# Linear attention with two expert stages on one core: y computed by tokens, the router's logits as eight more columns a head, one weight conversion at another place

## The chip, the cores and the metric

One core of one Trainium2 chip runs the whole program. TensorE (PE in the profile) multiplies into PSUM, VectorE (DVE), ScalarE (ACT) and GpSimd (POOL) work on the results, and SyncE (SP) issues most transfers. The metric is device time in microseconds (us), lower is better; where two numbers are compared, it is that of whole executions.

## The reference, cut to what matters

```
batch, n_heads, seq, head_dim = (4, 8, 768, 48)
f = 1.0 / (1.0 + np.exp(-f_logit))
for t in range(S):
    state = f[:, :, t, :, None] * state + np.einsum('bhd,bhe->bhde', k[:, :, t], v[:, :, t])
    y[:, :, t] = np.einsum('bhd,bhde->bhe', q[:, :, t], state)
x = np.ascontiguousarray(y.transpose(0, 2, 1, 3)).reshape(B * S, H * D)     # 3072 x 384
logits = x @ w_gate + modality_bias[modality_id]                            # 8 experts
e_idx = np.argmax(logits, axis=1)
out[mask] = gate_w[mask, None] * (np.maximum(x[mask] @ w1[e], 0.0) @ w2[e]) # for each expert e
return (1 / (1 + np.exp(-(x @ w_gate2))) * (x @ w_val)) @ w_out             # second stage, d_ff 1536
```

So there is a linear attention with a decay per feature, a top-1 mixture of eight experts that is routed by the attention's output, and a gated layer on all 3072 tokens.

## The kernel before, in words

The recurrence runs over 24 tiles of 128 tokens (6 chunks of 4 batches), in a loop whose iterations are called slots here. Heads stand in pairs: head 2·pr+j has 64 partitions, of which 48 differ. All products of this stage are in fp32, so each matmul instruction leaves two weight loads and two matmuls in the trace (a count of 16 there is 8 instructions). For tile i the names in the code and the profile are: `c` the running sum of the log decays (L966, 8 instructions), `rg` its two exponentials, `kqT` the decayed k and q, `turn` the transposed k (L1003, 4 transposes), `kt` its copy, `a` the products k·q (L1015, 16), `am` those after the causal mask, `u` the tile's contribution k·v to the state (L1033, 8), `s` the state.

The output y is made by features. `att_ys` (L1058, 8 instructions) multiplies the state with q, `att_y` (L1071, 8) adds v times `am`, both into the PSUM tile `yT`; ScalarE copies it (L1076); one slot later `att_x` (L1102, 8 instructions of 104 columns) multiplies the turned y with `wr`, which holds an identity and the router's weights side by side, and so gives both the rows by tokens and four partial logits a token. ScalarE copies these apart (`rows` L1105, `lg` L1106). The logits of a group of tiles (ROUTE) are summed on VectorE (`lgs`, L1108), and then a chain of small VectorE steps, dealt out one at a time between the other work (`tick`), finds expert, rank and place. Rows go to DRAM (`store_rows`), and a table of places is kept on chip.

The order of every engine is that of the code. A slot i issues a(i), ys(i-1), x(i-2), y(i-1), c(i+2), u(i), turn(i+1). The loads are issued in order by SP: f(i+5), kq(i+4), v(i+3), each into a ring of 4 or 5 buffers. Between them stand conversions of the last stage's float64 weights to float32 in halves: a load of 768 KB, one ScalarE step (L856), four VectorE steps (L861, L865, L869, L873), a store of 384 KB. CONV says in which slots of the recurrence one begins; others have their places in the expert stage.

The first two expert blocks (`slot32`, here block 0 and block 1) start from the tokens of the first 18 tiles: their ids are taken from the table (`take`, L351), their rows gathered from DRAM by POOL (`xg`, L403) and turned (`xT`, L739), while the last slots of the recurrence still run. After them come the other expert blocks and the gated layer.

Of the kernel before, what the change touches and what calls it, by code (L numbers as in the profile page):

```python
# [10 lines left out]
F32 = mybir.dt.float32  # L11
# [11 lines left out]
P = 128  # L23
# [5 lines left out]
E = 8  # L29
# [3 lines left out]
XW = 2 * D + E  # L33
# [10 lines left out]
CONV = (3, 7, 11, 15)  # L44
GROUPED = 17
PUT = (9, 13, 17)
# [14 lines left out]
def kernel(  # L61
# [3 lines left out]
    att_fv: bass.AP,  # L65
# [41 lines left out]
    wr = ctile([P, 4, XW], F32, "wr")  # L107
# [39 lines left out]
    def setup_early(causal):  # L147
# [12 lines left out]
        nc.gpsimd.memset(wr, 0.0)  # L160
        for j in range(2):
            nc.gpsimd.tensor_copy(
                out=wr[:, :, j * D:(j + 1) * D],
                in_=ident[:, 64 * j:64 * j + D].rearrange("p (o d) -> p o d", o=1).to_broadcast([P, 4, D]),
            )
# [7 lines left out]
    def load_router():  # L173
        wsrc = w_router.rearrange("(p j d) e -> j d p e", j=2, d=D)
        nc.sync.dma_start(out=wr[0:D, :, 2 * D:XW], in_=wsrc[0])
        nc.sync.dma_start(out=wr[64:64 + D, :, 2 * D:XW], in_=wsrc[1])

# [733 lines left out]
    def convert_last():  # L911
# [13 lines left out]
        [ap2.tile([P, 4 * D + 16], F32, name=f"s{b}{n}", tag=f"s{b}{n}", bufs=1) for n in range(2)] for b in range(B)  # L925
    ]

    def head(pr, j):
        return 2 * pr + (j ^ (pr & 1))

    def load_f(i):
        t = ap2.tile([P, TOK], F32, tag="f", name="f", bufs=4)
        nc.sync.dma_start(out=t, in_=att_fv[i, :, 0])
        st["f", i] = t
# [24 lines left out]
    def prep_c(i):  # L959

        nl = st.pop(("nl", i))
        ps = pool_a.tile([P, 4, P], F32, tag="c", name="c")
        for pr in range(4):
            for j in range(2):
                h = head(pr, j)
# [26 lines left out]
    def turn_bank(step):  # L992
        if ("turn", step) not in st:
            st["turn", step] = ps_t.tile([P, 512], F32, tag="t", name="turn")
        return st["turn", step]

    def att_k(i, step):
# [3 lines left out]
        ps = turn_bank(step)  # L1001
# [21 lines left out]

    def att_u(i):
# [4 lines left out]
        ps = ps_t.tile([P, 4, D], F32, tag="t", name="u")  # L1029
        for pr in range(4):  # L1030
            for j in range(2):
                f, h = 64 * (2 * pr + j), head(pr, j)
                nc.tensor.matmul(  # L1033
                    out=ps[64 * j:64 * j + 64, pr, :], lhsT=kt[:, f:f + 64], rhs=vt[:, h * D:h * D + D],
                    start=(pr == 0), stop=(pr == 3),
                )
        old, new = (s_sum[b][(c + n) % 2][:, 0:4 * D].rearrange("p (a d) -> p a d", a=4) for n in range(2))
        return state_steps(ps, old, new, g[:, :, P - 1:P].to_broadcast([P, 4, D]), c == 0)
# [10 lines left out]
    def att_ys(i):  # L1049
        c, b = i // B, i % B  # L1050
        qT = st.pop(("qT", i))
        ps = pool_y.tile([P, 2, 512], F32, tag="y", name="yT")
# [11 lines left out]
    def att_y(i):  # L1064
        c = i // B
        (am, _), vt, ps = st.pop(("am", i)), st.pop(("v", i)), st.pop(("y", i))
        for pr in range(4):
            for j in range(2):
                h = head(pr, j)
# [5 lines left out]
        yT = ap2.tile([P, 4, P], F32, tag="yT", name="yT")  # L1075
        nc.scalar.copy(  # L1076
# [793 lines left out]
```

## Time and profile before

| | |
|---|---|
| median of 3 runs | 839.23 us (837.32 to 841.04) |
| the profiled execution | 839.44 us, of which its span is 837.7 us |
| TensorE busy | 820.9 us, 98% of the span |
| VectorE busy | 456.7 us, 55% |
| ScalarE busy | 373.1 us, 45% |
| GpSimd busy | 189.0 us, 23% |

Times within the span are counted from its start. Busy shares are averages over stages: the recurrence ends at about 136 us of the span, and VectorE and ScalarE are far busier in it than later. A line number is that of the kernel before.

### The profile page before, as it was taken

The numbers are of one execution on the slowest core, as the hardware profiler recorded it, in microseconds if no ns is written. First come the engines' busy times: TensorE is split into PE (matmuls) and PEld (weight loads), VectorE is DVE, ScalarE is ACT, GpSimd is POOL, SyncE is SP. The second block draws the span as 40 slices with busy tenths as digits, with TensorE's granted clock in tenths as the row PEclk, the third lists the DMA queues.
The fourth block names the chain that finished last, engine by engine and source line by source line (L and its number), as shares of the span: only waits on it lengthen the run. The fifth ranks groups of instructions, "written<-read, shape, count | busy, mean of one in ns | idle before, by whom it ended". The sixth has DMA issues, their size and how long they took to land.

```text
span 837.7 us, 16650 instructions
## 1 busy us (share of the span) xinstructions
PE 820.9 (98%) x6533; PEld 740.5 (88%) x6533; DVE 456.7 (55%) x1046; ACT 373.1 (45%) x788; POOL 189.0 (23%) x277
## 2 busy tenths in 40 slices
PE   8999999999999999999999999999999999999995
PEld 7989986779999999998888888888888888888894
DVE  5899985758866777665673333324323423432221
ACT  6777762268756666565333222323322332223222
POOL 5311021234665654633001100200020020002002
PEclk9999999999999999999999999999999999999998
DMA  9878757849998788763140210120021011001001
GB/s 325 298 260 257 232 167 281 324 157 330 343 338 275 256 279 264 277 225 113 39 83 29 51 29 19 49 48 20 1 66 29 20 48 28 1 1 38 1 1 38
DMA packets 51414, 118.09 MB, mean 141 GB/s; under 512 B 20922, under 2 KB 33222, under 8 KB 51328
## 3 DMA queue, kind: packets, MB, share of 16 engines
q1 hardware_dynamic: 46336, 101.95, 36.7%
q0 software_dynamic: 4992, 15.00, 5.1%
q8 instruction: 53, 0.87, 0.4%
q14 instruction: 33, 0.27, 0.1%
HBM read 94.86 MB, written 18.53 MB: 135 GB/s over the span
## 4 chain that ended last, share of the span: by engine, by line
PE 76%; DVE 0%; ACT 0%; POOL 0%; issue 0%; DMA 0%; POOLq 0%; DVEq 0%; ACTq 0%
PE gv L1691 12%; PE gv L1692 12%; PE gv L1690 12%; PE y L746 10%; PE o L1720 6%; PE o L1718 6%; PE o L1719 6%; PE h L666 3%; PE h L669 3%; PE h L667 3%; PE xT L413 1%; POOL out_dram L1726 0%; DMA out_dram<-raw,tok 0%; PE h L764 0%; PE h L767 0%
## 5 line engine op out<-in xcount | busy, mean ns | idle before, releaser
L1706 DVE TENSOR_TENSOR sg<-sg,gv 128x256 f32<-128x256 f32 (+1 forms) x145 | 54.4, 416 | 247.3 <-PE gv L1692 247.3
L1704 ACT ACTIVATE sg<-gv 128x256 f32<-128x256 f32 (+1 forms) x145 | 47.8, 381 | 146.2 <-PE gv L1692 146.2
L1726 POOL DMA_INDIRECT out_dram<-raw,tok x24 | 23.6, 982 | 395.0 <-ACT raw L1723 387.4
L1707 ACT CAST gh<-sg 128x256 fp32r<-128x256 f32 (+1 forms) x145 | 53.6, 407 | 128.2 <-DVE sg L1706 128.2
L1709 DVE TENSOR_TENSOR gl<-sg,gh 128x256 fp32r<-128x256 f32 (+1 forms) x145 | 55.3, 422 | 11.6 <-ACT gh L1707 1.6
L673 DVE SCALAR_TENSOR_TENSOR hl<-h,hh 128x256 fp32r<-128x256 f32 x80 | 33.5, 421 | 38.9 <-ACT hh L672 37.8
L672 ACT ACTIVATE hh<-h 128x256 fp32r<-128x256 f32 x80 | 30.7, 385 | 49.4 <-PE h L669 49.4
L1692 PE MATMUL gv<-oddh,al 128*128 128x512 f32 (+1 forms) x120 | 44.3, 369 | 0.0
L1691 PE MATMUL gv<-oddl,ah 128*128 128x512 f32 (+1 forms) x120 | 44.3, 369 | 0.0
L1690 PE MATMUL gv<-oddh,ah 128*128 128x512 f32 (+1 forms) x120 | 44.1, 367 | 0.0
L1692 PE MATMUL gv<-oddh,bl 128*128 128x512 f32 x108 | 42.5, 394 | 0.0
L1692 PE MATMUL gv<-evenh,bl 128*128 128x512 f32 x108 | 42.5, 393 | 0.0
L1691 PE MATMUL gv<-oddl,bh 128*128 128x512 f32 x108 | 42.4, 393 | 0.0
L1691 PE MATMUL gv<-evenl,bh 128*128 128x512 f32 x108 | 42.4, 393 | 0.0
L1692 PE MATMUL gv<-evenh,al 128*128 128x512 f32 x108 | 42.3, 391 | 0.0
L1691 PE MATMUL gv<-evenl,ah 128*128 128x512 f32 x108 | 42.2, 391 | 0.0
L1690 PE MATMUL gv<-evenh,ah 128*128 128x512 f32 x108 | 42.0, 389 | 0.0
L1690 PE MATMUL gv<-evenh,bh 128*128 128x512 f32 x108 | 42.0, 389 | 0.0
L1690 PE MATMUL gv<-oddh,bh 128*128 128x512 f32 x108 | 42.0, 389 | 0.0
L403 POOL DMA_INDIRECT xg<-xd,ids x24 | 27.6, 1150 | 53.8 <-PE xT L413 29.1
L398 ACT CAST ah<-raw 128x1536 fp32r<-128x1536 f32 (+1 forms) x24 | 33.0, 1376 | 9.8 <-DVE raw L873 6.4
L990 POOL COPY gmin<-rg 128x4 f32<-128x4 f32 x24 | 16.0, 670 | 91.1 <-ACT rg L977 81.8
(369 smaller groups left out, 2378.4 us busy)
## 6 DMA issues: line engine op xcount, KB each, us to landing
raw<-in_w_dram SPq DMA_DIRECT2D x48, 768.0 KB
kq<-in_att_kq_dram SPq DMA_DIRECT2D x24, 512.0 KB
cvr<-in_w_glu_dram SPq DMA_DIRECT2D x10, 768.0 KB
f<-in_att_fv_dram SPq DMA_DIRECT2D x24, 200.0 KB
v<-in_att_fv_dram SPq DMA_DIRECT2D x24, 200.0 KB
x<-yd SPq DMA_DIRECT2D x12, 386.0 KB
raw<-in_w_glu_dram SPq DMA_DIRECT2D x6, 768.0 KB
raw<-wd SPq DMA_DIRECT2D x5, 768.0 KB
```

Source lines behind the costliest of these rows:

```text
L673: nc.vector.scalar_tensor_tensor(out=hl, in0=ps, scalar=0.0, in1=hh, op0=ALU.max, op1=ALU.subtract)
L746: nc.tensor.matmul(out=ps, lhsT=lhs[:, ts], rhs=rhs[:, fs], start=(g == 0 and part == 0), stop=(g == 7 and part == 2))
L1690: nc.tensor.matmul(out=ps[:, ns], lhsT=hi[:, sl], rhs=xh[:, c, ns], start=(c == 0), stop=False)
L1691: nc.tensor.matmul(out=ps[:, ns], lhsT=hi[:, sl], rhs=xl[:, c, ns], start=False, stop=False)
L1692: nc.tensor.matmul(out=ps[:, ns], lhsT=lo[:, sl], rhs=xh[:, c, ns], start=False, stop=(c == 2))
L1704: nc.scalar.activation(out=sg, in_=gate, func=AF.Sigmoid)
L1706: nc.vector.tensor_tensor(out=sg, in0=sg, in1=val, op=ALU.mult)
L1707: nc.scalar.copy(out=gh, in_=sg)
L1709: nc.vector.tensor_tensor(out=gl, in0=sg, in1=gh, op=ALU.subtract)
L1718: nc.tensor.matmul(out=ps, lhsT=gh[:, ts], rhs=hi[:, fs], start=(f == 0), stop=False)
L1719: nc.tensor.matmul(out=ps, lhsT=gh[:, ts], rhs=lo[:, fs], start=False, stop=False)
L1720: nc.tensor.matmul(out=ps, lhsT=gl[:, ts], rhs=hi[:, fs], start=False, stop=(f == 11))
```

## The change

Everything concerns the recurrence, but for one conversion.

- y is made by tokens: the masked products and q are the stationary operands, state and v the moving ones. `att_ys` and `att_y` have 16 instructions each with 56 columns, in place of 8 with 128. `att_x`, the copy `yT` and the identity in `wr` go away; the loop has one slot less (NT+1 in place of NT+2).
- v, the state and y have 56 columns a head: 48 values and 8 logits. The 8 columns of v are v times that head's rows of the router's weights, made by `att_w` from a second copy of v that the host lays out by features (`att_vt`, 192 KB a tile): 6 matmul instructions of 64 columns a tile, and a ScalarE copy into v's tile (`copy_w`). They stand behind y(i-1) and make tile i+1's columns. u has 56 columns, the state's two steps 224 in place of 192, and the logits' sum has 8 parts in place of 4.
- `wr` is now a block form of the router's weights, made by POOL with a copy and two selections (`setup_router`), from a load that moved to the front.
- Tile 0's and tile 1's columns are made ahead (`first_w`). c(1) has a PSUM tile of its own, so that c(0) and c(1) stand together.
- The logits of a tile are there one slot earlier, and the steps that follow were moved accordingly: PUT, CONV and the rank of tile 17's group (now at the end of slot 19, before in slot 20).
- CONV has three conversions, one slot earlier each, in place of four; the fourth moved to block 1 (load at its step 3, work at steps 6 and 7).

```diff
-CONV = (3, 7, 11, 15)
+CONV = (2, 6, 10)
-PUT = (9, 13, 17)
+PUT = (8, 12, 16)
...
+    def setup_router():
+
+        nc.gpsimd.tensor_copy(out=wr, in_=wl.to_broadcast([P, 3, H, E]))
+        for sign, base in ((1, 0), (-1, D - 1)):
+            nc.gpsimd.affine_select(
+                out=wr, in_=wr, pattern=[[sign * P, 3], [-sign * D, H], [0, E]], compare_op=ALU.is_ge, fill=0.0,
+                base=base, channel_multiplier=sign,
+            )
...
     def load_v(i):
-        vt = ap2.tile([P, TOK], F32, tag="v", name="v", bufs=5)
-        nc.sync.dma_start(out=vt, in_=att_fv[i, :, 1])
+        vt = ap2.tile([P, H, VW], F32, tag="v", name="v", bufs=5)
+        nc.sync.dma_start(out=vt, in_=att_v[i])
         st["v", i] = vt
+        turned = ap2.tile([P, 3, P], F32, tag="vt", name="vt", bufs=3)
+        nc.sync.dma_start(out=turned, in_=att_vt[i])
+        st["vt", i] = turned
...
+    def att_w(i, w):
+
+        turned = st.pop(("vt", i))
+        for c in range(3):
+            for t in range(2):
+                ts = slice(64 * t, 64 * t + 64)
+                nc.tensor.matmul(
+                    out=w[ts], lhsT=turned[:, c, ts], rhs=wr[:, c].rearrange("p h e -> p (h e)"), start=(c == 0),
+                    stop=(c == 2),
+                )
+        st["w", i] = w
+
+    def copy_w(i):
+        nc.scalar.copy(out=st["v", i][:, :, D:VW], in_=st.pop(("w", i)).rearrange("p (h e) -> p h e", h=H))
...
-                for j in range(2):
-                    rows, o = slice(64 * j, 64 * j + D), 64 * (j ^ (pr & 1))
+                for j, t in itertools.product(range(2), range(2)):
+                    rows, ts = slice(64 * j, 64 * j + D), slice(64 * t, 64 * t + 64)
                     nc.tensor.matmul(
-                        out=ps[o:o + 64, pr % 2, pr // 2 * P:pr // 2 * P + P], lhsT=s[rows, pr * D:pr * D + 64],
-                        rhs=qT[rows, pr, :], start=(pr < 2), stop=False,
+                        out=ps[ts, j, pr * VW:(pr + 1) * VW], lhsT=qT[rows, pr, ts], rhs=s[rows, pr, :],
+                        start=(pr == 0), stop=False,
                     )
...
-            for j in range(2):
-                h = head(pr, j)
-                o = 64 * (h % 2)
+            for j, t in itertools.product(range(2), range(2)):
+                ts = slice(64 * t, 64 * t + 64)
                 nc.tensor.matmul(
-                    out=ps[o:o + 64, pr % 2, pr // 2 * P:pr // 2 * P + P], lhsT=vt[:, h * D:h * D + 64],
-                    rhs=am[:, 4 * j + pr, :], start=(c == 0 and pr < 2), stop=(pr > 1),
+                    out=ps[ts, j, pr * VW:(pr + 1) * VW], lhsT=am[:, 4 * j + pr, ts], rhs=vt[:, 2 * pr + j, :],
+                    start=(c == 0 and pr == 0), stop=(pr == 3),
                 )
...
+        if i + 2 < NT:
+            att_w(i + 2, ps[:, 0, 256:256 + H * E])
...
-    for i in range(NT + 2):
+    for i in range(NT + 1):
...
         f2=[convert_mask, convert_high, convert_low, convert_store],
+        f3=convert_load,
         f4=[lambda: part(head, 0, 0), convert_mask, convert_high],
         f5=[lambda: part(head, 0, 1), convert_low, convert_store],
-        f7=load_n,
+        f6=[convert_mask, convert_high],
+        f7=[convert_low, convert_store, load_n],
```

What TensorE does in a slot of the middle of the recurrence, from one transposed k to the next, was this before (rows of its instructions in program order, with the output, the operands and how many of them follow each other):

```order
L1003 MATMUL turn<-ident,kqT 128x128 x4
L1015 MATMUL a<-kqT 64x128 x16
L1058 MATMUL yT<-kqT,s_143 64x128 x8
L1102 MATMUL turn<-wr,yT 64x104 x8
L1071 MATMUL yT<-am,v 64x128 x8
L966 MATMUL c<-causal,nl 64x128 x8
L1033 MATMUL u<-v,kt 64x48 x8
```

and it is this now:

```order
L1006 MATMUL turn<-ident,kqT 128x128 x4
L1018 MATMUL a<-kqT 64x128 x16
L1080 MATMUL y<-s_143,kqT 64x56 x16
L1092 MATMUL y<-v,am 64x56 x16
L1033 MATMUL y<-wr,vt 64x64 x6
L974 MATMUL c<-causal,nl 64x128 x8
L1055 MATMUL u<-v,kt 64x56 x8
```

The eight instructions of x are gone, ys and y have twice as many with 56 columns, and six short ones (w) came in behind y.

At the start, TensorE's order up to the second tile's products is now as follows (c(0) and c(1) are the 16 of one row, w of tile 0 stands ahead of the first transposes, w of tile 1 ahead of a(1)):

```order
L1277 MATMUL warm<-zeros 128x256 x4
L974 MATMUL c<-causal,nl 64x128 x16
L1033 MATMUL w<-wr,vt 64x64 x6
L1006 MATMUL turn<-ident,kqT 128x128 x4
L1018 MATMUL a<-kqT 64x128 x16
L974 MATMUL c<-causal,nl 64x128 x8
L1055 MATMUL u<-v,kt 64x56 x8
L1006 MATMUL turn<-ident,kqT 128x128 x4
L1033 MATMUL w<-wr,vt 64x64 x6
```

Before, the same row of 16 c stood there too, and no w. At the end, TensorE's order from slot 22 into block 0 (`h` are its first products, `gps` a check of the decays) was this:

```order
L1015 MATMUL a<-kqT 64x128 x16
L1058 MATMUL yT<-kqT,s_143 64x128 x8
L1102 MATMUL turn<-wr,yT 64x104 x8
L1071 MATMUL yT<-am,v 64x128 x8
L1418 MATMUL gps<-ident,gm_2715 1x128
L739 MATMUL xT<-ident,xg 128x128 x6
L1058 MATMUL yT<-kqT,s_145 64x128 x8
L1102 MATMUL turn<-wr,yT 64x104 x8
L1071 MATMUL yT<-am,v 64x128 x8
```

and it is this now, from the last row of the rank of tiles 18 to 21, which has moved ahead of the turned rows:

```order
L290 MATMUL rank<-ebase,ones 128x32
L744 MATMUL xT<-ident,xg 128x128 x6
L1431 MATMUL gps<-ident,gm_3046 1x128
L1080 MATMUL y<-s_145,kqT 64x56 x16
L718 MATMUL h<-raw_120,eh_2798 128x256 x3
L1092 MATMUL y<-v,am 64x56 x16
L718 MATMUL h<-raw_120,eh_2798 128x256 x6
```

Block 0's first products now stand ahead of the last y; before, they stood behind it, with the last x between them and the rest of block 0.

## Rows read from the trace of the kernel before

**Rows 1.** The page, part 1: busy time of each engine.

```profile
PE 820.9 (98%) x6533; PEld 740.5 (88%) x6533; DVE 456.7 (55%) x1046; ACT 373.1 (45%) x788; POOL 189.0 (23%) x277
```

**Rows 2.** Stretches: recurrence, its end, blocks 0 and 1 (start:end, length, busy).

```profile
9.63:110.00 100.37, 99.96 (x2218) 91.26 (x2219) 90.78 (x233) 74.26 (x161) 23.50 (x56) 1.00 0.83 276
110.00:140.00 30.00, 27.81 (x501) 23.24 (x498) 21.10 (x99) 13.94 (x36) 7.12 (x14) 1.00 0.65 239
140.00:180.00 40.00, 39.58 (x169) 28.43 (x167) 26.52 (x93) 11.71 (x25) 7.60 (x8) 1.00 0.56 212
```

**Rows 3.** Timeline of TensorE, one slot (start, length until its last end).

```profile
68.58 1.10 PE L1015 MATMUL a<-kqT 48*64 48x128 f32 x32
69.50 0.62 PE L1058 MATMUL yT<-kqT,s 48*64 48x128 f32 x16
70.05 0.94 PE L1102 MATMUL turn<-wr,yT 128*64 128x104 f32 x16
70.81 1.04 PE L1071 MATMUL yT<-am,v 128*64 128x128 f32 x16
71.69 1.04 PE L966 MATMUL c<-causal,nl 128*64 128x128 f32 x16
72.56 0.62 PE L1033 MATMUL u<-v,kt 128*64 128x48 f32 x16
73.11 0.44 PE L1003 MATMUL turn<-ident,kqT 128*128 128x128 f32 x2
```

**Rows 4.** The same of slot 1, where y follows a directly.

```profile
12.72 1.10 PE L1015 MATMUL a<-kqT 48*64 48x128 f32 x32
13.76 1.09 PE L1071 MATMUL yT<-am,v 128*64 128x128 f32 x16
14.68 1.04 PE L966 MATMUL c<-causal,nl 128*64 128x128 f32 x16
```

**Rows 5.** Line L1015 in two stretches of 0.05 us: PE, then PEld (count).

```profile
63.45:63.50 0.05, 0.04 (x4) 0.04 (x4) 1.00 0.50 178
63.50:63.55 0.05, 0.05 (x4) 0.05 (x8) 1.00 0.80 312
```

**Rows 6.** Four slots (columns as rows 2), and VectorE's only wait in them.

```profile
58.19:79.54 21.35, 21.35 (x479) 19.52 (x478) 20.12 (x56) 15.68 (x35) 3.28 (x5) 1.00 0.82 261
...
DVE s L1044 <- PE u L1033: 1.1, 2, 0.8
```

**Rows 7.** Groups of VectorE and ScalarE from 30.77 to 106.13 us.

```profile
L1076 ACT COPY yT<-yT 128x512 f32<-128x512 f32 x14 | 8.2, 587 | 4.4 <-PE yT L1071 4.4
L1105 ACT COPY rows<-turn 128x384 f32<-128x384 f32 x14 | 6.7, 481 | 8.8 <-PE turn L1102 8.8
L1046 DVE TENSOR_TENSOR s<-s,rg 128x192 f32<-128x192 f32 x15 | 5.3, 357 | 0.0
L1106 ACT COPY lg<-turn 128x32 f32<-128x32 f32 x14 | 2.7, 192 | 0.0
L1108 DVE TENSOR_REDUCE lgs<-lg 128x32 f32<-128x128 f32 (+1 forms) x4 | 1.4, 361 | 0.1
```

**Rows 8.** Transfers from 20 to 105 us, and SP's wait ahead of v's loads.

```profile
DMA packets 9885, 22.42 MB, mean 264 GB/s; under 512 B 969, under 2 KB 6839, under 8 KB 9863
...
SPq L943 <- PE yT L1071: 13.6, 14, 1.5
```

**Rows 9.** Timeline of TensorE at the start.

```profile
5.12 1.71 PE L966 MATMUL c<-causal,nl 128*64 128x128 f32 x16
8.02 1.09 PE L966 MATMUL c<-causal,nl 128*64 128x128 f32 x16 [1.19 <-ACT rg L977]
9.04 0.66 PE L1003 MATMUL turn<-ident,kqT 128*128 128x128 f32 x4
```

**Rows 10.** Timelines of POOL and TensorE at the end of the recurrence.

```profile
123.33 1.25 POOL L403 DMA_INDIRECT xg<-xd,eids  x1 [0.17 <-issue]
...
129.05 0.52 PE L739 MATMUL xT<-ident,xg 128*128 128x128 f32 x3 [0.40 <-DMA xg<-xd,eids]
130.03 0.52 PE L739 MATMUL xT<-ident,xg 128*128 128x128 f32 x3 [0.46 <-DMA xg<-xd,eids]
```

**Rows 11.** VectorE's longest wait from 159 to 182 us, late in block 1.

```profile
DVE xtl L416 <- ACT xth L415: 4.3, 2, 3.3
```

More of the change, by code (lines that the diff above doesn't have):

```diff
@@ L990, in prep_mul, with att_k @@
         nc.gpsimd.tensor_copy(out=gmin[:, i, :], in_=rg[:, 1, :, P - 1])
[L992 to L997, printed above, removed]
+    def att_k(i):
         if i // B == NCH - 1:
@@ L1000, in att_k @@
         kT = st["kT", i]
-        ps = turn_bank(step)
+        ps = ps_t.tile([P, 512], F32, tag="t", name="turn")
         for j in range(4):
@@ L1097, in att_x @@
         lg, rows = st["lg"], st["rows", first_i]
-        ps = turn_bank(step)[:, 0:4 * XW].rearrange("p (a x) -> p a x", a=4)
-        for pr in range(4):
-            for t in range(2):
-                ts = slice(64 * t, 64 * t + 64)
-                nc.tensor.matmul(
-                    out=ps[ts, pr, :], lhsT=yT[:, pr, ts], rhs=wr[:, pr, :], start=(pr == 0), stop=(pr == 3)
-                )
-        nc.scalar.copy(out=rows[:, j, 0:DM].rearrange("p (a x) -> p a x", a=4), in_=ps[:, :, 0:2 * D])
-        nc.scalar.copy(out=st["lg4"][:, j], in_=ps[:, :, 2 * D:XW])
+        ps = ps[:, :, 0:4 * VW].rearrange("p j (a x) -> p j a x", a=4)
+        nc.scalar.copy(out=rows[:, j, 0:DM].rearrange("p (a j d) -> p j a d", a=4, j=2), in_=ps[:, :, :, 0:D])
+        nc.scalar.copy(out=st["lg4"][:, j].rearrange("p (a j) e -> p j a e", j=2), in_=ps[:, :, :, D:VW])
+        if i + 2 < NT:
+            copy_w(i + 2)
         if j == n - 1:
@@ L1114, in att_x, with open_rows @@
             )
+    group_of = {i: (a, n) for a, n in ROUTE for i in range(a, a + n)}
+    def open_rows(i):
+        first_i, n = group_of[i]
+        t = ap2.tile([P, 4, ROW], F32, tag="rows", name="rows")
+        nc.gpsimd.tensor_copy(out=t[:, 0:n, DM + 1].bitcast(I32), in_=tokid[:, first_i:first_i + n])
+        st["rows", first_i] = t
     def late_at(first_i, n):
@@ L1310 @@
     to_store = due = None
[L1311 removed]
+    for i in range(NT + 1):
         routed = due
[L1313 removed]
+        due = i - 1 if i and sum(group_of[i - 1]) == i else None
         if due is not None and due >= NE - 3:
@@ L1409 @@
         if i + 1 < NT:
-            att_k(i + 1, i)
+            att_k(i + 1)
         if i + 3 < NT:
             prep_l(i + 3)
-        if i == GROUPED + 1:
-            convert_more()
-            half_done.clear()
+        if i < NT:
+            ticking(state)
         if i == NT - 1:
+            ps_a.close()
+            ps_mm = psum.enter_context(tc.tile_pool(name="ps_mm", bufs=3, space=PSUM, side="right"))
+            turn_x(early_x[0])
             gps = ps_t.tile([1, P], F32, tag="lg", name="gps", bufs=1)
@@ L1422 @@
             nc.vector.tensor_scalar(out=flag_i, in0=gm2, scalar1=0.5, scalar2=None, op0=ALU.is_lt)
-        if i < NT:
-            ticking(state)
-        if i == NT - 1:
-            ps_a.close()
-            ps_mm = psum.enter_context(tc.tile_pool(name="ps_mm", bufs=3, space=PSUM, side="right"))
-            turn_x(early_x[0])
-        if i != NT:
+        if i != NT - 1:
             to_store = NE - 4 if i == NE else routed if routed != NT - 3 else None
-        if i == NE + 1:
-            while "oh" not in st["oh", NE - 3]:
-                tick()
         if i == NE + 2:
```

139 lines of the change are left out of this document (64 added, 75 removed).

## The prediction

> **What bounds the kernel now.** First the busy times: TensorE is busy for 98% of the span, no other engine for more than 55% [rows 1]. Then the same by stretches, since shares mix stages. In the recurrence TensorE is busy for 99.96 of 100.37 us, but VectorE for 90.78 too. At its end, from 110 to 140 us, TensorE is idle for 30.00 - 27.81 = 2.2 us; in blocks 0 and 1 it is full again [rows 2]. So a microsecond that leaves TensorE in the recurrence leaves the total, as long as VectorE, the closest follower, keeps up, and as long as nothing at the end stands still by the clock. The granted clock is at its upper level (1.00, so 2.4 GHz) in every one of these stretches, and TensorE stays as busy as before, so the clock does not enter.
>
> **TensorE, per tile.** I price by starts, since ends overlap: a row's cost is the next row's start less its own. In one slot that gives a 0.92, ys 0.55, x 0.76, y 0.88, c 0.87, u 0.55 us [rows 3].
>
> Two edges are in these numbers. Where a (48 rows by 64 columns, four tiles of the array at once) is followed by 128-row products, it costs 1.04 instead of 0.92 [rows 4, 3]: 0.11 for closing one tiling, and it sits at the end of ys and u. y behind a costs 0.92, behind x 0.88 [rows 4, 3]: 0.05 for opening; today x pays it.
>
> Removed: x, 0.76.
>
> w: 6 instructions of 128 rows by 64 columns, with 64 moving columns. The nearest row is u, 8 such with 48 columns. If only columns counted, c (128 columns, 0.87) and x without its opening (104 columns, 0.71) give 0.0066 us a column for 8 instructions, so 0.34 at 48; u takes 0.44 without its closing and 0.55 with it. So short products have a floor, 0.055 to 0.069 us an instruction. I take 0.058, near the lower end, because w, y and c stand in one tiling and don't close: w costs 0.35 (bounds 0.33 and 0.41).
>
> y: 16 instructions with 56 columns, by the same floor 16 x 0.058 = 0.93, and it now pays the opening: 0.98 against 0.88, so +0.10 (bounds +0.05 and +0.28).
>
> ys: 16 instructions of 48 by 64 with 56 columns. The row is a: 16 of this kind with 128 columns in 0.92, so they cannot cost more than 0.92 + 0.11 = 1.03. If the loads of four tiles go side by side, four instructions cost what u's pairs cost, 4 x 4 x 0.029 = 0.47, with the closing 0.58. In a's first 0.05 us four loads have begun, in the next 0.05 eight are under way, on four tiles [rows 5]; in u the loads of two tiles do the same work in the time of one. So I take 0.58 against 0.55: +0.03 (bounds 0 and +0.48).
>
> u: 56 columns lie under the floor, 0 (at most 8 x 0.0066 = +0.05).
>
> Sum: -0.76 + 0.35 + 0.10 = -0.31 for 24 tiles, +0.03 for the 20 tiles with a state: -7.4 + 0.6 = **-6.8 us** (bounds, the four worst or best together: -0.38 and +0.46 a tile).
>
> The Trainium skill has a rule against this, in "TensorE: Matmul & The Clock Gate", Part 3, "The mechanism": a weight load runs beside running matmuls only where it goes to other row groups. w and y load all rows. By that rule their loads would stand open; it is the third rival below, and u's row speaks against it.
>
> **The other engines in the recurrence.** ScalarE loses yT (587 ns) and keeps rows and lg [rows 7]; it gains a copy of 64 elements, at most lg's 192 ns plus a little. It is idle for over 5 us in four slots [rows 6] and stays behind TensorE: nothing. What would be late next is ys, since y's PSUM tile is single: its copies must end before ys of the next slot, some 3 us behind y (c, u, turn, a stand between: 0.87 + 0.55 + 0.58 + 0.92). They take about 0.9.
>
> VectorE is the narrow one. In four slots it is busy 20.12 of 21.35 us and waits 1.1 for u [rows 6]. The state's two steps grow from 192 to 224 columns: from 357 ns by at most the ratio 224/192, +0.06 each; one row does not tell its fixed part, so I take half, +0.03. The logits' sum doubles its input: 361 ns and at most double; I take +0.13. Per four slots +0.4, so 20.5 us, against TensorE's 21.35 - 4 x 0.28 = 20.2. They meet. But VectorE's waits for u vanish when it is the later one, and its products are used late: turn wants kqT about a slot after the rg that feeds it. A lag of 0.3 us per four slots, over the three conversions (slots 2 to 13), is under 1 us. Behind slot 13 the fourth conversion is gone from VectorE (four steps), and it catches up. So nothing, with the second rival for the case that it isn't.
>
> Transfers: v's rows grow by 12% and vt adds 192 KB a tile, so 0.22 MB more a slot, less 1.2 MB for the conversion that leaves. From 20 to 105 us the mean is 264 GB/s [rows 8]; in four slots with a conversion it becomes about 6.6 MB in 20.2 us, 326 GB/s. SP issues v and vt only when y of an older tile frees a buffer (its wait is 13.6 us in 14 times [rows 8]), but that is three slots ahead of w, so a landing may come some 10 us late unseen. Nothing; the fourth rival prices it.
>
> **The start.** TensorE waits 1.19 us between c(0) and c(1) for the exponentials [rows 9]. Now c(1) has its own bank, and w(0) stands behind it, in that gap, if the router's load and vt(0) are there; POOL's copy and selections must be done too. If so, w(0)'s 0.35 lies in idle time: **-0.35** (0 if POOL or the load comes late).
>
> **The end.** The two x behind slot 23 are in the sum already. What is open is the idle time of 2.2 us. POOL issues the gather at 123.33, and TensorE waits 0.40 and 0.46 for it at 129.05 and 130.03 [rows 10]. TensorE gets there earlier now: slots 22 and 23 lose about 0.9 us (0.28, and 0.62 where x goes and no w is left). If the gather lands as long after its issue as before, this 0.9 is waited out. But nearly 6 us for it is long: the first weights of block 0 are under way then. The rank of tile 17's group moves from slot 20 to slot 19, so these weights are asked for earlier, and the gather has the queues more to itself. Between +0.9 and -2.2 (all idle gone) I take the middle, **-0.7**.
>
> **The conversion in block 1.** Four VectorE steps and one ScalarE step at steps 6 and 7, where VectorE waits 4.3 us in two times, 3.3 us at once [rows 11]. They fit, or nearly: 0. Without that cover it would delay the turned rows of the next block by at most those steps, about 3 us. Its load goes out on SP behind the store of step 2, in a stretch where SP has little to send.
>
> Sum: -6.8 - 0.35 - 0.7 = -7.85. The profiled execution took 839.44 us, 0.2 above the median of 839.23, so I predict 839.44 - 7.85 = **831.6 us**.
>
> **Rivals.**
> 1. VectorE becomes the bound in slots 2 to 13. Then these 12 slots keep their length (20.5 of work plus 1.1 of waits for u is 21.6 against 21.35) and only 12 of 24 tiles give their 0.28: 839.44 - 3.4 - 1.0 = 835.0. For it: 20.12 of 21.35. Against it: a slot of slack between the two engines. 0.15.
> 2. The loads of four tiles do not go side by side. ys then costs up to 1.03, +0.48 on 20 tiles: +9.0, so 840.6, no change. Against it: rows 5. It decides from the point where ys costs 0.9. 0.07.
> 3. Loads stay open in front of short products. Then each of y's and w's instructions pays load and columns one after the other, 0.055 for the load and 56 x 0.0066 / 8 = 0.046 for the columns (0.053 at 64): y 1.62 with 0.05 for the opening, w 0.65. Per tile -0.76 + 0.65 + 0.79 + 0.03 = +0.71, so +17, 856, slower. It decides from 0.08 an instruction on. Against it: u at 48 columns would cost 8 x (0.055 + 0.040) = 0.76 and costs 0.55. 0.03. This is what the rule of the Trainium skill above would do; by u's row the trace does not bear it out.
> 4. Transfers limit the slots with conversions. At 300 GB/s four slots need 22.0 us instead of 20.2, three times: +5.3, so 836.9. For it: the mean of 264 leaves out pauses. Against it: the depth of three slots. 0.08.
> 5. More comes: the end loses all its idle time, and VectorE's catching up shortens slots 20 and 21, where today it is nearly full: 829 and below. 0.07.
>
> The forecast itself, 828.5 to 834.5: 0.60.
>
> **The numbers.** 0.5% is 4.2 us, about what a measurement of this kernel can tell from no change: faster means below 835.0, slower above 843.4. Faster is the forecast, rival 5 and half of rival 1: 0.60 + 0.07 + 0.08 = 0.75. Within it: the other half of rival 1, rival 4, and 0.02 of rival 2: 0.17. Slower: rival 3 and the rest of rival 2, with stalls added to it: 0.08. The range leaves out rivals 2 and 3 and the far ends of 4 and 5: 828.0 to 837.0.
>
> **What would show it.** In the middle of the recurrence, starts of a 4.85 us apart where they were 5.12; w 0.35, y 0.98, ys 0.58, u 0.55 by starts. A ys near 1.0 is rival 2; y above 1.2 is rival 3. VectorE busy without a pause, with TensorE waiting for kqT or am ahead of turn or y, is rival 1; TensorE waiting for vt, or copy of w late for u, is rival 4. TensorE's wait at xT of 0 to 1.8 us sizes the last term. The forecast fails if slots come out at 5.1 or longer.

## The result and the profile after

The changed kernel takes **849.5 us** (median, 846.6 to 851.5) where the kernel before, run beside it, takes 838.65: the ratio is 1.0127, with an interval of 1.0109 to 1.0146. It is slower by 10.9 us, and faster by 7.8 was forecast.

First the busy time of TensorE on the page (part 1), which answers to [rows 1]:

```profile
PE 817.9 (96%) x7141; PEld 740.0 (87%) x7141; DVE 459.4 (54%) x1038; ACT 363.3 (43%) x788; POOL 184.6 (22%) x277
```

TensorE is busy for 3.0 us less, with more instructions (7141 records for 6533), and stands still for longer. Where, the stretches tell (start:end, length, busy PE, PEld, DVE, ACT, POOL, granted clock, DMA share, GB/s); the first answers to [rows 2], the others are the two longest waits, each with what comes behind it:

```profile
9.83:121.00 111.17, 97.85 (x2686) 89.98 (x2686) 91.25 (x239) 65.60 (x158) 19.23 (x53) 0.98 0.86 287
...
73.60:76.35 2.75, 0.22 (x8) 0.15 (x4) 1.64 (x4) 1.01 (x2) 0.62 (x1) 1.00 1.05 295
76.35:80.50 4.15, 4.15 (x87) 3.82 (x86) 3.79 (x9) 1.56 (x3) 0.00 (x0) 0.64 0.61 178
...
118.85:122.21 3.36, 0.23 (x6) 0.09 (x3) 1.45 (x4) 0.00 (x0) 0.19 (x1) 0.95 0.16 55
122.21:126.50 4.29, 4.29 (x79) 4.20 (x82) 0.85 (x4) 2.19 (x7) 0.34 (x1) 0.64 0.36 102
```

In the recurrence TensorE is idle for 13.3 of 111.2 us; before it was 0.4 of 100.4. Behind each of the two longest waits it runs for over 4 us at a granted clock of 0.64, a mixture of its two levels, 1.2 and 2.4 GHz. All of the loss lies ahead of block 0: its first h starts at 144.02 instead of 132.99, and from there to the end it is 704.8 us against 704.7.

The timeline of TensorE in the changed kernel (start, length until its last end; in brackets the idle time ahead and what ended it); it answers to [rows 3, 4, 9]:

```profile
5.12 2.29 PE L974 MATMUL c<-causal,nl 128*64 128x128 f32 x32
8.75 0.57 PE L1033 MATMUL w<-wr,vt 128*64 128x64 f32 x12 [1.34 <-POOL gmin L998]
...
17.24 0.57 PE L1033 MATMUL y<-wr,vt 128*64 128x64 f32 x12 [1.12 <-DMA vt<-in_att_vt_dram]
17.64 1.05 PE L974 MATMUL c<-causal,nl 128*64 128x128 f32 x16
18.52 0.63 PE L1055 MATMUL u<-v,kt 128*64 128x56 f32 x16
19.07 0.66 PE L1006 MATMUL turn<-ident,kqT 128*128 128x128 f32 x4
19.66 1.10 PE L1018 MATMUL a<-kqT 48*64 48x128 f32 x32
...
37.69 0.62 PE L1055 MATMUL u<-v,kt 128*64 128x56 f32 x15
40.25 0.26 PE L1055 MATMUL u<-v,kt 128*64 128x56 f32 x1 [1.94 <-issue]
...
41.17 1.10 PE L1018 MATMUL a<-kqT 48*64 48x128 f32 x32
42.10 0.64 PE L1080 MATMUL y<-s,kqT 48*64 48x56 f32 x32
42.67 1.15 PE L1092 MATMUL y<-v,am 128*64 128x56 f32 x32
43.64 0.53 PE L1033 MATMUL y<-wr,vt 128*64 128x64 f32 x12
44.00 0.60 PE L974 MATMUL c<-causal,nl 128*64 128x128 f32 x7
45.73 0.71 PE L974 MATMUL c<-causal,nl 128*64 128x128 f32 x9 [1.13 <-issue]
...
122.91 2.02 PE L974 MATMUL c<-causal,nl 128*64 128x128 f32 x16
124.62 0.99 PE L1055 MATMUL u<-v,kt 128*64 128x56 f32 x16
...
144.02 0.48 PE L718 MATMUL h<-raw,eh 128*128 128x256 f32 x1
```

Read by starts, the prices are those of the prediction: a 0.93, ys 0.57, y 0.97, w 0.36, c 0.88, u 0.55, turn 0.59, in all 4.85. But TensorE stops in the middle of u, with one record of 16 still to come, and in the middle of c, with nine to come. It waits for nothing that the trace shows: no semaphore, no transfer. The view of its waits, from 12 to 144 us, sums them up (total, times, longest):

```profile
PE u L1055 <- issue: 4.5, 2, 2.5
PE y L1092 <- issue: 4.4, 2, 3.1
PE y L1033 <- issue: 1.7, 1, 1.7
PE c L974 <- issue: 1.1, 1, 1.1
...
PE a L1018 <- issue: 0.8, 1, 0.8
PE y L1080 <- issue: 0.6, 1, 0.6
```

13.1 us of waits named "issue", which I call unnamed waits from here on. The wait for vt at 17.24 is not among them. The kernel before has one of 0.3 and, at its end, another of 0.3.

**Where they fall.** They stand at the matmul records 596, 723, 849, 975, 1605, 2235, 2741 and 3248, that is, 126 records or a multiple of 126 apart, within three. 126 matmuls, as many weight loads and a few records of synchronisation make about 256 instructions (between the first four of these places lie 257, 255 and 256 records of TensorE in all). In the transfers there is a queue of its own for instructions (q8 in the list of queues), with packets of 16384 bytes. The records of both, side by side, for waits that follow each other directly (in the kernel before, the block's start is counted back, 126 matmul records from the wait):

```
kernel    block starts   next packet under way   TensorE goes on
after        34.23          37.84 to 38.80           40.25
after        40.25          43.40 to 44.35           45.73
after        45.73          49.23 to 50.31           51.83
before       46.38          49.71 to 51.09           52.57
```

The kernel before has the same thing, once: a stops behind 8 of its 32 records at 51.81 and goes on at 52.57, a wait of 0.30 us by the view of its waits. So a block of 256 instructions is used up, and the packet with the next one has not come. A packet takes about 1 us, and at each of the eight places of the changed kernel TensorE goes on 1.2 to 1.5 us behind its end. (The wait of 0.25 us at the end of the kernel before, at 126.19, is no such case: the last packet had ended 4.5 us ahead of it.)

The blocks without a wait say the same. Counted in steps of 256 records, the changed kernel has 25 blocks from 11 us to its first h. In the eight whose next packet began 2.95 us or more behind the block's start, a wait followed; in the 17 in which it began after 2.65 us or less, none did. How late a packet begins goes with the data under way: where the transfers' engines were busy for at most 0.7 of the 3 us behind the start it was 0.8 us in the median (9 blocks), above 0.85 it was 2.8 (16 blocks). The kernel before has six packets that began 2.9 to 3.4 us behind their block, and only one of them was waited for, by 0.30 us.

The Trainium skill, "Runtime: NRT & Kernel Launch", section "Instruction fetch mechanics", describes it: instructions are refilled in blocks of 16 KiB, 256 instructions, by a queue that the sequencer drives itself. The trace agrees in the size and in the place. The section calls the cost "mostly hidden"; here it is 13.1 us, and the measurement decides.

### The profile page after: what moved, and what is told of

The parts are those of the page before. It is cut to its first block, busy times and chain, and to the rows that moved or that the text cites. A ratio compares the mean times of both kernels' runs of the same rounds, so it can differ in the third digit from the quotient of the medians.

```text
span 848.8 us, 17921 instructions
## 1 busy us (share of the span) xinstructions
PE 817.9 (96%) x7141; PEld 740.0 (87%) x7141; DVE 459.4 (54%) x1038; ACT 363.3 (43%) x788; POOL 184.6 (22%) x277
## 4 chain that ended last, share of the span: by engine, by line
PE 75%; DVE 0%; ACT 0%; POOL 0%; issue 0%; DMA 0%; POOLq 0%; ACTq 0%; DVEq 0%
PE gv L1698 12%; PE gv L1699 12%; PE gv L1697 11%; PE y L751 10%; PE o L1727 6%; PE o L1725 6%; PE o L1726 6%; PE h L671 3%; PE h L674 3%; PE h L672 3%; PE xT L418 1%; POOL out_dram L1733 0%; DMA out_dram<-raw,tok 0%; PE h L769 0%; PE h L772 0%
## 5 line engine op out<-in xcount | busy, mean ns | idle before, releaser
L998 POOL COPY gmin<-rg 128x4 f32<-128x4 f32 x24 | 13.6, 566 | 98.2 <-ACT rg L985 98.2
```

## Experiments

**Theory F**: TensorE's next block of instructions comes too late, for two reasons together: the changed kernel uses a block up faster (144 matmul records in a plain slot of 4.85 us, so 126 in 4.2, where it was 116 in 5.12, so 126 in 5.6), and the packet waits behind more data. Its rivals: **T**, the added transfers alone; **R**, the number of instructions alone; **W**, a wait for vt or for the copy of w that the trace fails to name. (The expectations count 148 and 120 records a slot: with the products of the router's rank, which some slots have besides.)

The numbers of all runs, to be read beside what follows. The records and the length are those of a plain slot, read by starts; a block is 126 records at that pace, GB/s are from 20 to 105 us, the unnamed waits are those from 12 to 125 us, h is the start of block 0's first h. The runs come from several series, each with the kernel before in it (838.4 to 839.8), so totals are compared by the ratios; vt_three and a_still are one run each.

| kernel | records a slot | slot | block | GB/s | unnamed waits | h at | time | ratio to before |
|---|---|---|---|---|---|---|---|---|
| before | 116 | 5.12 | 5.6 | 264 | 0.3 | 132.99 | 838.65 | |
| after | 144 | 4.85 | 4.2 | 292 | 11.8 | 144.02 | 849.5 | 1.0127 (1.0109 to 1.0146) |
| vt_three | 144 | 4.85 | 4.2 | 254 | 8.9 | 140.04 | routing differs | |
| a_still | 144 | 4.85 | 4.2 | 71 | 1.6 | 130.02 | routing differs | |
| b_load | 116 | 5.12 | 5.6 | 315 | 1.3 | 133.68 | 840.2 | 1.0017 (1.0007 to 1.0026) |
| a_pace | 146 | 5.48 | 4.7 | 281 | 3.9 | 145.89 | 852.0 | 1.0160 (1.0142 to 1.0178) |
| a_whole | 128 | 5.06 | 5.0 | 296 | 4.0 | 136.16 | 842.1 | 1.0046 (1.0028 to 1.0063) |
| a_ys_whole | 112 | 5.28 | 5.9 | 307 | 0.3 | 136.03 | 841.9 | 1.0032 (1.0017 to 1.0046) |
| y_w_whole | 122 | 6.16 | 6.4 | 275 | 0 | 153.08 | 859.5 | 1.0243 (1.0226 to 1.0260) |
| b_halves | 148 | 5.53 | 4.7 | 257 | 1.1 | 144.58 | 851.4 | 1.0147 (1.0130 to 1.0164) |
| b_halves2 | 148 | 5.27 | 4.5 | 258 | 2.5 | 143.22 | 850.3 | 1.0153 (1.0128 to 1.0178) |
| a_kq96 | 144 | 4.85 | 4.2 | 244 | 10.4 | 150.71 | 856.6 | 1.0190 (1.0173 to 1.0207) |
| a_store4 | 144 | 4.85 | 4.2 | 268 | 10.8 | 143.37 | 850.3 | 1.0133 (1.0119 to 1.0148) |
| a_spread | 144 | 4.85 | 4.2 | 233 | 5.8 | 149.03 | 855.5 | 1.0185 (1.0155 to 1.0216) |

### Data without instructions, instructions without data

**vt_three** loads vt for three tiles only.

```diff
-        turned = ap2.tile([P, 3, P], F32, tag="vt", name="vt", bufs=3)
-        nc.sync.dma_start(out=turned, in_=att_vt[i])
+        if i < 3:
+            turned = ap2.tile([P, 3, P], F32, tag=f"vt{i}", name="vt", bufs=1)
+            nc.sync.dma_start(out=turned, in_=att_vt[i])
+            st["vt", i] = turned
+        else:
+            st["vt", i] = st["vt0", i % 3]
```

> The changed kernel, with vt loaded for tiles 0 to 2 only; later tiles reuse these three, so the router's right half of the sum is that of other tokens and the expert loads differ: only the recurrence is read, up to the first h of block 0 (144.02 in the changed kernel, 132.99 before). TensorE's instructions are the same; 192 KB a tile less is carried. Theory F (TensorE runs out of instructions: a block of 256 is used up in about 4.2 us, and the packet with the next block comes late, the later the more data is under way): the stalls without a named cause (13.1 us in the changed kernel) go down to 4 to 9, the first h at 135 to 140. Rival T (traffic alone): stalls below 2, first h at 128 to 132. Rival R (the number of instructions alone): stalls stay at 11 to 15, first h at 142 to 146. Rival W (a wait for vt or for the copy of w that the trace does not name): stalls gone, since vt has landed long before.

8.9 us of unnamed waits are left, and h comes at 140.04, at the upper end of F. T had asked for less than 2 and W for none, since vt had long landed. R's range for the waits, 11 to 15, is missed as well.

**b_load** is the counterpart: the kernel before with vt's bytes and none of its instructions.

```diff
         nc.sync.dma_start(out=vt, in_=att_fv[i, :, 1])
+        more = ap2.tile([P, 3, P], F32, tag="vt", name="vt")
+        nc.sync.dma_start(out=more, in_=att_vt[i])
```

> The kernel before, with a load of 192 KB a tile added behind v's load, into a ring of two tiles that nothing reads. TensorE's instructions are those of before, 120 records a slot; the traffic is about that of the changed kernel. Theory F: a block lasts 5.3 us here, a packet may come over 1 us later than in the changed kernel before TensorE notices; stalls of 1 to 4 us in all, so 840 to 843. Rival T (traffic alone): stalls as in the changed kernel, 849 to 853. Rival R (number of instructions alone): no stall more than before, 838 to 840.

TensorE's unnamed waits from 12 to 125 us:

```profile
PE u L1036 <- issue: 0.9, 1, 0.9
PE yT L1061 <- issue: 0.4, 1, 0.4
```

More is carried than in the changed kernel (315 GB/s for 292), and 1.3 us of waits come of it, at a ratio of 1.0017. T is refuted. More data alone does nearly nothing as long as a block lasts 5.6 us.

**a_still** goes to the other end: all instructions of the change, nearly no loads.

```diff
     def load_kq(i):
+        if i >= 4:
+            st["kq", i] = first_kq[i % 4]
+            return
```

and the like for f, v and vt.

> The changed kernel with the same instructions on TensorE, but f, kq, v and vt are loaded for the first tiles only (f and kq 4, v 5, vt 3) and used again by the later ones: it leaves out nearly all of the recurrence's loads, so the routing differs and only the recurrence is read (first h of block 0: 144.02 in the changed kernel, 132.99 before). What stays are the stores of rows and the conversions. Theory F with both causes (a packet with instructions waits behind data): with the DMA engines mostly idle a packet starts about 1 us after its block, so 1.0 + 1.0 + 1.45 = 3.5 us are needed of the 4.2 that a block lasts; stalls under 3 us in all, slots of 4.85, first h at 126 to 131. Rival R (the number of instructions alone sets the stalls, whatever else is carried): stalls of 10 us and more, first h at 140 to 145.

The stretch from 20 to 105 us, TensorE's unnamed waits from 12 to 125, one more wait, the first h, and the stretch ahead of the longest wait:

```profile
20.00:105.00 85.00, 81.86 (x2368) 76.53 (x2361) 79.02 (x213) 57.36 (x140) 13.97 (x26) 1.00 0.21 71
...
PE y L1106 <- issue: 1.3, 1, 1.3
...
PE a L1032 <- issue: 0.3, 1, 0.3
...
69.22 0.66 PE L1020 MATMUL turn<-ident,kqT 128*128 128x128 f32 x4 [0.94 <-PE u L1069]
...
130.02 1.56 PE L718 MATMUL h<-raw,eh 128*128 128x256 f32 x6
...
44.83:48.21 3.38, 3.38 (x96) 3.15 (x96) 3.38 (x10) 2.66 (x7) 0.20 (x1) 1.00 0.79 269
```

With the engines of the transfers at 0.21 instead of 0.89, the same instructions finish 14.0 us earlier than in the changed kernel and 3.0 earlier than before. R is refuted in its pure form, and so is the rest of W, for the copy of w is still there. The waits are 1.6 us, or 2.5 with the one at 69.22, which the view puts down to u: it stands at a multiple of 126 records and 1.55 us behind a packet's end. Behind the two blocks whose start a wait marks (50.58 and 69.22) the next packet began after 1.40 and 1.18 us; in the changed kernel it was 3.15 to 3.62 in the rows side by side above, and 5.1 ahead of the stop at 122.21. The longest wait confirms it from the other side: its packet began at 48.21, 3.4 us behind the block's start (44.83, counted back), and in these 3.4 us the engines were at 0.79 again. So both halves of F are needed: the pace of the instructions makes the time short, and the data ahead of the packet uses it up.

### The pace of the instructions

**a_pace** adds work and next to no instructions: one product of 384 columns a tile.

```diff
+        nc.tensor.matmul(
+            out=ps[0:64].rearrange("p a t -> p (a t)")[:, 0:384], lhsT=nl[:, 0:64], rhs=zeros, start=True, stop=True
+        )
         for pr in range(4):
```

> The changed kernel with one product more a tile, 128 by 64 with 384 columns of zeros, in front of c and into c's bank, which c then overwrites: result and traffic the same, 0.65 us of work a tile by c's price (0.218 for 128 columns), 24 times, and nearly no instruction more. If the stalls had nothing to do with how fast instructions are used up, the total would grow by 24 x 0.65 = 15.7, to 865. Theory F: a block now lasts 4.7 us instead of 4.2, the stalls fall by 6 to 10 us, and the total grows by only 6 to 10: 855 to 860.

A slot by starts, and the unnamed waits from 12 to 125 us:

```profile
63.12 1.10 PE L1021 MATMUL a<-kqT 48*64 48x128 f32 x32
...
68.02 0.19 PE L284 MATMUL rank<-oh,before 128*128 128x32 bf16 x1
...
68.19 0.64 PE L1009 MATMUL turn<-ident,kqT 128*128 128x128 f32 x4
68.75 1.10 PE L1021 MATMUL a<-kqT 48*64 48x128 f32 x32
...
PE y L1036 <- issue: 2.5, 1, 2.5
PE y L1095 <- issue: 1.4, 1, 1.4
```

The slot takes 5.63 less 0.17 for rank, 0.6 more than 4.85: over 13 us in 22 to 24 tiles. The whole kernel grows by 2.5, or 2.8 by the ratios. The rest came back out of the unnamed waits, 3.9 for 11.8 up to 125 us and 4.8 for 13.1 up to 144, and out of the clock (0.99 for 0.98 from 10 to 150 us, some 1.5 us). The waits fell as F had it, by 6 to 10; its total, 855 to 860, was too high. This is the plainest sign: TensorE was not short of time but of instructions.

**a_whole** and **a_ys_whole** use fewer instructions for the same products.

```diff
-            for j, t in itertools.product(range(2), range(2)):
-                rows, ts = slice(64 * j, 64 * j + D), slice(64 * t, 64 * t + 64)
-                nc.tensor.matmul(out=ps[ts, j, pr, :], lhsT=kT[rows, pr, ts], rhs=qT[rows, pr, :], start=True, stop=True)
+            for j in range(2):
+                rows = slice(64 * j, 64 * j + D)
+                nc.tensor.matmul(out=ps[:, j, pr, :], lhsT=kT[rows, pr, :], rhs=qT[rows, pr, :], start=True, stop=True)
```

In a_ys_whole ys is cut in the same way.

> The changed kernel with only a in 8 instructions of 48 by 128: 132 records a slot, a block lasts 4.6 us. Same traffic and result. Theory F: stalls between those of the changed kernel (13.4) and of a_ys_whole, 5 to 9 us, total 841 to 846 if a stays at 0.92. Rival T: 848 to 852.

> The changed kernel with a and ys in 8 instructions each (48 rows by 128 columns, the two row halves in turn) where there are 16 of 48 by 64: the same traffic and result, 116 matmul records a slot instead of 148 (120 before). What a wider weight load costs is bounded by rows: y and w of 128 by 128 cost 0.229 and 0.257 us an instruction in y_w_whole, which is about 0.13 of load in front of 56 columns; there every load went to the rows in use. Here the next load goes to the other row half. If it lies beside the products, a stays at 0.92 and ys at 0.57; if it doesn't, each gains about 0.13 x 8 / 2 = 0.5. Theory F with loads beside the products: a block of 256 lasts 5.3 us, stalls of 2 to 6 us instead of 13.4, total 834 to 841. Rival T (traffic sets the stalls): stalls of 10 us and more, 846 to 852. With loads that stand open: stalls small, but 24 us more work, 850 to 862.

a_whole's 842.1 lies in F's range, but not by F's terms: a costs 1.09 and ys 0.62 by starts (62.95, 64.04, 64.66), not 0.92 and 0.57, some 5 us more work, and the waits fell further than to 5 to 9, to 4.0 us up to 125. (A wait of 0.92 at 37.17 that the view puts down to ScalarE comes on top: it ends 1.45 us behind a packet's end, at the place of a block's start.) In a_ys_whole the waits are gone (0.3 us), while the traffic is the highest of the changed kernels, 307 GB/s. But its time went into prices, in its timeline:

```profile
60.16 1.16 PE L1018 MATMUL a<-kqT 48*128 48x128 f32 x16
61.15 1.00 PE L1080 MATMUL y<-s,kqT 48*128 48x56 f32 x16
62.08 1.15 PE L1092 MATMUL y<-v,am 128*64 128x56 f32 x32
```

a 0.99 and ys 0.93, for 0.92 and 0.57: 0.07 in 24 tiles and 0.36 in 20, 8.9 us. Its longest waits from 12 to 125 us are now for other engines' work:

```profile
PE y L1080 <- ACT v L1040: 1.1, 1, 1.1
PE a L1018 <- DVE di L302: 0.8, 1, 0.8
```

With the instructions in time the prediction's sum holds to a microsecond: it put h at 132.99 - 6.8 - 0.35 = 125.8, and 125.8 + 8.9 + 1.1 + 0.8 + 0.3 = 136.9; measured 136.03. The total, 841.9, lies just above F's 834 to 841: the loads neither lay beside the products nor stood open in full.

**y_w_whole** does the same with y and w.

```diff
-            for j, t in itertools.product(range(2), range(2)):
-                ts = slice(64 * t, 64 * t + 64)
+            for j in range(2):
                 nc.tensor.matmul(
-                    out=ps[ts, j, pr * VW:(pr + 1) * VW], lhsT=am[:, 4 * j + pr, ts], rhs=vt[:, 2 * pr + j, :],
+                    out=ps[:, j, pr * VW:(pr + 1) * VW], lhsT=am[:, 4 * j + pr, :], rhs=vt[:, 2 * pr + j, :],
```

> The changed kernel with y in 8 instructions and w in 3, of 128 by 128 instead of 128 by 64: the same result and traffic, 126 records a slot instead of 148. Prices from rows: by columns (c: 128 columns in four pairs, 0.87) y costs 0.76, by the turn's floor (0.147 an instruction of 128 by 128) 1.18; now 0.97. w 0.32 to 0.44, now 0.36. Another closing of a tiling of 0.1 may come in. Theory F: a block lasts 4.9 us instead of 4.2, the stalls fall from 13 to 5 to 9 us: 841 to 847 with y and w at their present price. Rival T and rival W: stalls stay, 848 to 852. Rival R: stalls near those of before (126 records against 120), 833 to 838.

```profile
64.00 1.99 PE L1088 MATMUL y<-v,am 128*128 128x56 f32 x16
65.83 0.84 PE L1031 MATMUL y<-wr,vt 128*128 128x64 f32 x6
66.60 0.66 PE L974 MATMUL c<-causal,nl 128*64 128x128 f32 x8
```

A miss on the price: y 1.83, w 0.77. Two instructions with 64 columns of weights that follow each other cost 0.122 together (0.97 / 8), one with 128 columns 0.229. The waits are gone, but the blocks now last 6.4 us, so it says nothing against the rivals that a_ys_whole doesn't say better.

**b_halves** and **b_halves2** give the kernel before about the number of instructions that the change has, at its own traffic.

```diff
-                nc.tensor.matmul(
-                    out=ps[o:o + 64, pr % 2, pr // 2 * P:pr // 2 * P + P], lhsT=vt[:, h * D:h * D + 64],
-                    rhs=am[:, 4 * j + pr, :], start=(c == 0 and pr < 2), stop=(pr > 1),
+                for t in range(2):
+                    f = pr // 2 * P + 64 * t
+                    nc.tensor.matmul(
+                        out=ps[o:o + 64, pr % 2, f:f + 64], lhsT=vt[:, h * D:h * D + 64],
+                        rhs=am[:, 4 * j + pr, 64 * t:64 * t + 64], start=(c == 0 and pr < 2 and t == 0),
```

ys likewise; b_halves2 turns the two inner loops round (t outside, j inside).

> The kernel before, with y and ys each in 16 instructions of 64 moving columns where there are 8 of 128: the traffic and the result of before, 32 records a slot more. By the floor of 0.058 us an instruction (u, w and y bear it out) TensorE's own work grows by about 0.05 for y and 0.03 for ys, 2 us in all: 841. Theory F: a block now lasts about 4.3 us instead of 5.3, and stalls come on top, 3 to 8 us: 844 to 849. Rival T: 840 to 842 without stalls. Rival R: 850 to 855, stalls of about 13 us.

> The kernel before with y and ys in 16 instructions of 64 columns as in b_halves, but in an order in which neighbours go to different tiles: in b_halves two neighbours share one, and y came to 1.10, ys to 0.69, u to 0.60 by starts, 0.4 us a slot more, which is nearly all of its 12 us; its blocks lasted 4.6 us and stalled only three times. Now y at 0.95 to 1.0, ys at 0.57, 152 records a slot of 5.2 us, a block lasts 4.3 us at the traffic of before. Theory F with both causes: stalls of 3 to 7 us, total 845 to 850. Rival R (number alone): stalls of about 13 us, 854. Rival T: stalls as before, 841 to 843.

b_halves is no test of the pace: in its order two neighbours use the same tile, y costs 1.10, ys 0.68, and its 12 us are mostly work: 851.4 lies in R's range, but with 2.4 us of unnamed waits up to 144 where R had about 13. b_halves2 has y at 0.94 and ys at 0.64, which is 0.06 in 24 tiles and 0.09 in 20, 3.2 us more than before, and unnamed waits of 5.6 us up to 144, at 850.3 the edge of what F expected. Behind two of the waits the granted clock fell as well (0.98 from 10 to 150 us). So the pace alone brings waits into the kernel before too, fewer than in the changed kernel; its blocks last 4.5 us and it carries less, which fits F.

### Attempts on the data, which missed

**a_kq96** was to carry 11% less, **a_store4** to cut the largest bursts, **a_spread** to do both.

```diff
-        nc.sync.dma_start(out=t, in_=att_kq[i])
+        if i < 4:
+            nc.sync.dma_start(out=t, in_=att_kq[i])
+        else:
+            for j in range(2):
+                nc.sync.dma_start(out=t[64 * j:64 * j + D], in_=att_kq[i, 64 * j:64 * j + D])
```

```diff
             if i + 1 in PUT:
-                store_rows(i - 4)
+                first_i, n = group_of[i - 4]
+                t = st.pop(("rows", first_i))
+                pieces[:] = [(first_i + j, t[:, j]) for j in range(n)]
+            store_piece()
```

> The changed kernel with its instructions untouched; from tile 4 on kq's load carries only the 96 rows that are used (the pads keep older, finite values), 128 KB of 1.13 MB a tile less, in two loads. Same result. Theory F (a packet with instructions waits for the data that is queued ahead of it, and that counts the more the faster instructions are used up): stalls fall from 13.4 to 9 to 12 us, total 845 to 849. By instruction number alone nothing changes: 849 to 851.

> The changed kernel with the four-tile stores of rows in the grouped slots cut into one piece a tile, sent a slot apart (three rows buffers for two; to make room v has 4 for 5, kt and lg4 one each). The traffic is the same, the burst of 772 KB is gone. In the changed kernel four stalls, 1.96, 2.75, 0.86 and 3.36 us by starts, 8.9 of 13.4 us, lie at packets that came while such a store was being carried. Theory F with bursts: these stalls halve or more, total 842 to 847. If bursts do not matter, only the mean traffic and the number of instructions: 848 to 852.

> a_store4 and a_kq96 together; besides, the load of a conversion (768 KB) in two halves a slot apart, and vt(2) asked for before f(4) and kq(3), since TensorE waits 1.12 us for it at 17.24 in the changed kernel. TensorE's instructions are those of the changed kernel. Theory F with bursts: stalls of 3 to 6 us, total 836 to 841, at or under the kernel before. If bursts do not matter: 846 to 849.

a_kq96 got slower than the changed kernel by 7 us, or 5 by the ratios. Its stretch from 20 to 105 us:

```profile
20.00:105.00 85.00, 74.90 (x1940) 69.44 (x1938) 65.94 (x168) 48.47 (x116) 10.97 (x22) 0.92 0.90 244
```

The engines are busy as in the changed kernel (0.90 for 0.89) and move 244 GB/s instead of 292: its packets of 4096 bytes took 0.246 us in the median instead of 0.159, so it took fewer bytes and no engine time away. The waits stayed (10.4), and some grew so long that the granted clock of that stretch is 0.92 for 0.98, which alone is 85 x 0.06 = 5 us. As a dose of less data it failed, and so did a_spread, which contains it, and in which TensorE waited 3.6 us for kqT at 31.82; that its other order of the first loads did this is not shown.

a_store4 is a fair test, and what I had read into the trace fell: four of the longest waits lay beside stores of rows, but without these bursts the waits come to 10.8 us, at other places. Which data a packet waits behind is thus not settled, only that it waits long where much is under way and briefly where little is. No version of these beat the kernel before; a_ys_whole came nearest among the changed ones, at 1.0032.

## Why the prediction was wrong

**The step that failed** is the first one: "a microsecond that leaves TensorE in the recurrence leaves the total, as long as VectorE, the closest follower, keeps up", and with it "TensorE stays as busy as before, so the clock does not enter". TensorE had another supplier, the packets with its own instructions, and the sum had no term for them: 28 more matmul records a slot in less time. It cost 13.1 us of waits and 3.2 us of lower clock behind them, where 6.8 us of work were saved. The kernel before showed it at 52.57 in its timeline:

```profile
51.81 0.45 PE L1015 MATMUL a<-kqT 48*64 48x128 f32 x8
52.57 0.89 PE L1015 MATMUL a<-kqT 48*64 48x128 f32 x24 [0.30 <-issue]
```

A run of one instruction form, cut in two, with nothing waited for: a block that came late even when they lasted 5.6 us. The prediction passed over it. None of the five rivals had this mechanism.

**The sum with it.** By its terms for the tiles and the start h was forecast at 125.8. Add the unnamed waits, 13.1 less the 0.6 that the kernel before already had; 1.1 for vt(2) at 17.24; 0.55 at the start (TensorE's first a came 0.20 later, not 0.35 earlier); and the lower clock behind the two longest waits, 4.15 x 0.36 + 3.5 x 0.06 + 4.29 x 0.36 = 3.2 (the 3.5 us from 80.50 have 0.94). That is 143.2; measured 144.02. Smaller terms are not in it: the last y now stands behind h (0.97 less), no wait for xT is left (0.86 less), and other named waits grew by 0.9 (0.43 for am at 13.94 and 0.76 for oh, where it was 0.30). With them it is 142.2, so nearly 2 of the 11 us have no name here.

**The prices were right.** Slot 4.85 as forecast; w 0.36 for 0.35, y 0.97 for 0.98, ys 0.57 for 0.58, u 0.55. Rivals 2 and 3 are refuted: four tiles load side by side, and loads don't stand open in front of short products, as long as neighbours go to different tiles. That is the limit of it: with neighbours in one tile (b_halves) y costs 1.10 where it is 0.94 in b_halves2, and with loads of full width (y_w_whole) it costs 1.83. The rule of the Trainium skill, "TensorE: Matmul & The Clock Gate", Part 3, "The mechanism", does not hold for y and w as the change writes them: all rows are loaded, and y costs 0.97 where that rule gave 1.62. (The sum of rival 3 has the opening on top, 1.67.)

**VectorE is not the bound** (rival 1): in the changed kernel it waits for u itself. Its groups from 30 to 108 us, with ScalarE's copy of w, answer to [rows 7]:

```profile
L1068 DVE TENSOR_TENSOR s<-s,rg 128x224 f32<-128x224 f32 x13 | 5.1, 389 | 0.0
L1066 DVE TENSOR_TENSOR s<-s,u 128x224 f32<-128x224 f32 x13 | 4.9, 379 | 7.1 <-PE u L1055 7.1
L1040 ACT COPY v<-y 128x64 f32<-128x64 f32 x13 | 3.0, 230 | 0.0
L1112 DVE TENSOR_REDUCE lgs<-lg 128x32 f32<-128x256 f32 (+1 forms) x4 | 2.4, 593 | 2.3 <-ACT lg L1108 2.3
```

The state's step grew by 0.03 as taken (357 to 389 ns); the sum of the logits by 0.23 instead of 0.13, which nothing waits for.

**Transfers**: that a landing may come late unseen was right in the middle and wrong at the start, where vt(2) has no slots of lead yet: 1.1 us. As a limit on the slots (rival 4) they did not show: with more than the change carries b_load loses 1.4 us. What I did not see is that the same engines carry TensorE's instructions.

**The start**: c(1) follows c(0) directly, as the change has it, but w(0) waits 1.34 us for POOL behind it. **The end**: TensorE came to xT without a wait, where it was 0.86 before, as the term of -0.7 had it; but the waits ahead gave the gather that time, so it can't be read apart. **The conversion in block 1** shows no cost: from h on both kernels take the same, though the changed one has its last y there too.

## What to carry to other kernels

Where an engine is nearly full, divide its instructions by its time before the change and after: a change that trades few long instructions for many short ones may use up a block of 256 faster than the next one comes, and then each microsecond saved comes back as a wait. The sign is a run of one form cut in two, with "issue" in the brackets, at equal distances in instructions; the queue of the instructions in the transfers tells the rest. Price such a change by its instructions and by the data under way together: neither alone showed the loss here.

## What the runs showed of the hardware

- In the changed kernel a packet of instructions began 0.8 us behind its block in the median where the transfers' engines were busy for at most 0.7 of the next 3 us, and 2.8 where it was above 0.85, at most 5.1. It takes about 1 us, and where TensorE waited for it, it went on 1.2 to 1.5 us behind its end.
- A wait of 2.5 or 3.1 us is paid twice: behind it TensorE ran 4.15 and 4.29 us at a granted clock of 0.64, c 1.71 instead of 0.88 by starts.
- Two instructions with 128 rows by 64 columns of weights in neighbouring tiles and 56 moving columns cost 0.122 us; one with 128 by 128 costs 0.229.
- Loading 96 of 128 rows in two loads of 48 took the engines as long as all 128 in one: 244 GB/s at a share of 0.90, 292 at 0.89.
